# Seven block products for a third group's output, and the weight sums on GpSimd issued earlier

## The chip, the cores and the metric

The kernel runs on one core of one Trainium2 chip. The metric is the device time of one execution in microseconds (us), taken as the median of repeated runs. Engines are named as the profile names them: PE is TensorE (matmul; PEld its weight loads), DVE is VectorE, ACT is ScalarE, POOL is GpSimd, SP is the engine that issues most DMAs.

## The reference

A gated linear attention over 4 batches, 8 heads, 768 positions and a head width of 48, whose output, seen as 3072 tokens of 384 values, goes through an RMS norm and a gated expert layer with 1536 hidden values:

```python
state = np.zeros((B, H, D, D))
for t in range(S):
    state = alpha[:, :, t, :, None] * state + np.einsum('bhd,bhe->bhde', k[:, :, t], v[:, :, t])
    y[:, :, t] = np.einsum('bhd,bhde->bhe', q[:, :, t], state)
x = y.transpose(0, 2, 1, 3).reshape(B * S, H * D)          # (3072, 384)
xn = x / np.sqrt(np.mean(x * x, axis=-1, keepdims=True) + 1e-06) * rms_g
g = xn @ w_gate                                            # (3072, 1536)
out = (g * (1 / (1 + np.exp(-g))) * (xn @ w_val)) @ w_out  # (3072, 384)
```

## The kernel before

**Tiling.** The 3072 tokens are cut into 24 chunks of 128 (number cc; six per batch, the four batches in turn), and the chunks into seven groups of 4, 2, 2, 4, 4, 4 and 4 (`GROUPS`, numbered 0 to 6). Every float32 product is made of three float16 matmuls (`SPLIT`): each operand is split into a high half and the rest, and high x high, high x rest and rest x high are added up in PSUM.

**Stages.** `attention(cc)` does one chunk. VectorE scans the decay forward and back (L730), and multiplies k and q with the scans (L753, L760). The halves are made by ScalarE (high) and VectorE (rest: L808 for q). PE makes the score matrix `at2`. VectorE masks it (L886), ScalarE takes its high half `a16`, and VectorE the rest (L911, `al` in the plan). PE adds the chunk's y from the state (L924) and from the scores (L941), and the new state sums (L959). VectorE scales y by the norm's gains (L1001), GpSimd takes the root of the norm (L997, tile `ss`, one tiny instruction per chunk), and the split x is turned by a DMA. `decode` brings one block of the weights, which arrive as 64-bit floats, into float16 halves; six blocks i0 to i11 (gate and value) and o0 to o5 (output) make up 18 in all. A name in `SIGN_H` has its sign bits copied by ScalarE and one VectorE instruction at L544 in place of two at L531 and L536; a name in `LOW_W` has its rest made by PE and ScalarE instead of VectorE. `inspect` loads blocks once more and checks their range.

**The expert layer.** `expert_in(g, f)` makes 128 of the 1536 hidden values (step f, twelve of them) of a group: 9 matmuls for the gate and 9 for the value (L1215, 512 columns wide for a group of four chunks), SiLU on ScalarE, the gating on VectorE (L1232), the split on ScalarE and VectorE (L1245). `expert_out` makes the output of groups 0 to 4: per chunk 12 x 3 matmuls of 384 columns (L1593), so 144 for a group of four. Groups 5 and 6 (`FAST`) use `fast_out`: the product of h (512 x 1536) and w_out (1536 x 384) as 2 x 2 blocks with seven block products in place of eight (L1474), 252 matmuls of 192 columns for a group. For that, `mix(g, i)` makes sums and differences of the halves of two h tiles on VectorE (L1297 to L1326: per pair of steps five instructions of 256 columns and one of 512 more than the plain split) and `mix_out(i)` makes sums of w_out's blocks on GpSimd: nine instructions for each of six blocks, 54 in all (L1384, L1390, L1393, L1403; five of the nine are 384 wide, four are 192 wide; their tiles are `kh_t`, `qp_t` and the results `raw_T` and `wu_T`).

**Order.** A planner lists all operations with their dependences, and each engine issues its own in the order that the number table `PLACE` gives. Nothing moves at run time: an instruction whose operands are late holds all that stand behind it on its engine. `BUFS` says how many buffers each name has. `WARM` and `FILL` are numbers of filler matmuls at the start.

Of the kernel before, what the change touches and what calls it, by code (L numbers as in the profile page):

```python
# [8 lines left out]
F16 = mybir.dt.float16  # L9
F32 = mybir.dt.float32  # L10
# [46 lines left out]
SIGN_H = ["i0", "i1", "i2", "i4", "i5", "i6", "i7", "i8", "i9", "i10", "i11", "o0"]  # L57
REST_A = ['i0', 'i1', 'i2', 'i4']
WARM = 11
FILL = 16  # L60
LOW_W = ["i6", "o1", "o2"]

BUFS = dict(
    att=3, v=2, ss=2, kh=2, qp=2, k16=2, q16=2, kT=2, v16=4, gd=2, a16=2, s16=2, dk=1, x32=1, x16=2,
    xT=2, raw=4, wu=2, h16=13, sl=2, h32=3, ob=2, at2=1, y=2, mm=4,
# [3 lines left out]
    rg=0.7, resta=1.06, warm=6.4, fill=0.22, hneg=0.23, hr=0.5,  # L69
    ss=0.12, kh2=0.68, scu=1.1, st2=0.34, scan1=0.6, xs=0.5, xh=0.45, xless=0.17, xr=0.46, kid=0.98, kTh=0.65, kTl=0.53, xid=0.88, xTl=0.47, kneg=0.23, kr=0.45,  # L70
# [5 lines left out]
    neg=0.48, wneg=0.2, wl2=0.38,  # L76
# [19 lines left out]
9 0 5 30 8 v 2b 6 2 3 1b u 2f w 11 2c 3a 1 4 7 c h 1l f g i l j p n 13 16 z 14 1c 1k 1o 1q 1w 21 27 2e 2i 2l 18  # L96
1d 1f a b k r x 10 y 12 17 15 1e 1i 1m 1u 1y 24 25 28 2g 2m 2t 2v 2z 1r 1v 1x d q 19 1g 2o 1h 1j 20 1n 1t 22 2a
2r 2w 3i 3l 3q 3g 42 49 4f 2k 32 38 s 2d 8w 2s 2x 3o 31 35 3d 3n 4a 3h 3r 3v 3z 44 46 4c 4l 4t 4y 51 4r 5n 67 t
36 3p 3u 40 45 o 2u 34 39 3e 3k m 1z 26 2j 2p 2y e 1p 1s 23 2h 2n 29 3t 3w 41 4b 4p 2q 4i 4m 53 58 5r 3y 4z 52
54 5b 5l 6q 6t 5d 5q 6b 70 3f 64 6c 6p 6v 72 4q 5z 61 69 6h 6m 6w 82 85 8f 8l 92 59 6y 7g 7n 7y 86 5h 78 7b 7h  # L100
7o 7s 7l 8y 94 9e 9i 9p 6f 7d 7w 7z 8n 8z 96 9c 84 8h 8p 9d 7q 8m 8u 9f 9z a7 aa ae a3 a5 ac al 8s a4 a6 ab ag
ay 8k 9s af ak an b9 9j b0 b4 bh bm bq 4e 4j 4s 5a 5f 5k 3s 43 48 4d 4h 57 33 37 3b 3j 5j 5m 3c 47 3m 4g 4k 4u
4x 50 55 5p 6s 6u 56 6l 5e 6z 76 79 5c 5o 5t 5v 63 6d 5i 5u 5x 68 7e 7j 6i 6r 6n 7f 83 8b 6e 77 74 7p 7t 89 5y
62 6a 6k 6o 75 7i 7r 7u 8j 99 9m 81 87 8c 91 9r a0 6x 7a 7k 80 8e 98 97 9l 9o 9w ah bf 8r 90 93 9g 9v bl 8g ai
8v bd bg bx 9t 9x a2 ad ap b2 b7 bc bi bp by c5 cc cg ds mq co cr c9 cf cl ct dc gr 1a 4n 3x 4o 5s 4w 5w 5g 8i
at 73 7c 7x av az 9a 9k 9n 9q aj b6 b8 bb bn br bv c0 c1 c6 c7 cb cd ci aw bt c2 cn 4v 71 60 66 65 6g 8q 8d 8x
9b a1 ao 8o 95 9h 7m 88 8a 8t am aq 9u 9y a8 ar au ax ba be bk bo bs bw bz c3 b5 cz d8 dg d3 d9 db dm e5 e8 d0
# [36 lines left out]
1au 1b0 1b3 19q 19y 19z 1a6 1a5 1a8 1ad 1ac 1ag 1ai 1ao 1aa 1an 1al 1az 1b4 1bh 1bu 1c3 1cd 1a4 1a9 1ae 1aj 1ap
1ar 1aw 1as 1av 1ay 1bd 1ax 1b2 1b5 1b8 1b1 1bj 1b7 1bb 1bc 1ba 1bf 1bg 1be 1bm 1bl 1bq 1br 1bp 1bt 1bs 1bw 1du
1bv 1cp 1dw 1bx 1c8 1dy 1ak 1bi 1at 1bo 1bn 1by 1c2 1cc 1bz 1c0 1c1 1c5 1c6 1c7 1ca 1c9 1cv 1cg 1cs 1d1 1d3 1cl
1cm 1co 1ce 1cr 1cu 1d5 1c4 1cb 1ci 1cj 1ch 1d7 1dc 1dn 1cf 1ck 1cn 1cx 1cw 1cz 1de 1d2 1dg 1dl 1dp 1d0 1d6 1df
1dk 1dm 1dr 1eg 1em 1eu 1cq 1ct 1da 1dd 1cy 1d4 1d8 1di 1dv 1dx 1e3 1dz 1ee 1e5 1e8 1dq 1ds 1e4 1ef 1eh 1db 1dh
1dj 1eb 1do 1dt 1e0 1e2 1ej 1el 1en 1eq 1f6 1es 1ex 1e9 1ez 1eo 1et 1ev 1e1 1e6 1e7 1ep 1ec 1ei 1ek 1f1 1f3 1f5
# [6 lines left out]
class Plan:  # L156
# [21 lines left out]
    def order(self):  # L178
# [9 lines left out]
        for o in done:  # L188
# [11 lines left out]
            if o["lock"]:  # L200
                port, owner = t + (0.1 if o["lock"] == 2 else cost), e
# [145 lines left out]
def tile_attn_moe(  # L347
# [1540 lines left out]
```

## Time and profile before

| | us |
|---|---|
| three runs | 505.33, 504.17, 505.94 (median 505.33) |
| the profiled execution, its own time | 504.43 |
| its span in the trace | 502.7 |
| PE busy | 494.9 |
| VectorE busy | 426.4 |
| ScalarE busy | 290.8 |
| GpSimd busy | 75.6 |

The span runs from the first to the last instruction that the profiler records; 1.7 us of the execution lie outside it. The rows that are read from this execution stand in a section below.

### The profile page before, as it was taken

The page shows a single profiled execution, that of the slowest core. Times are in us where ns is not written, and L with a number is a line of the kernel's source. Part 1 is how long each engine was busy: PE and PEld are TensorE (multiplying, and loading weights), DVE is VectorE, ACT ScalarE, POOL GpSimd, SP SyncE. Part 2 cuts the span into 40 slices and gives each one's busy share as a digit, 9 for nine tenths or more (in the row PEclk, how much of TensorE's full clock was granted, in tenths as well). Part 3 has the DMA queues.
Part 4 walks back from the last instruction along what each step waited for, and adds up shares of the span by engine and source line. Part 5 has one row for each costly group of instructions (what it writes and reads, how often), then busy time and mean ns, then how long its engine had stood idle before and what let it go on. Part 6 is the DMA issues. An engine that isn't in the chain of part 4 may idle for free.

```text
span 502.7 us, 13364 instructions
## 1 busy us (share of the span) xinstructions
PE 494.9 (98%) x5483; PEld 319.1 (63%) x5483; DVE 426.4 (85%) x805; ACT 290.8 (58%) x793; POOL 75.6 (15%) x109
## 2 busy tenths in 40 slices
PE   8999999999999999999999999999999999999996
PEld 4888645668968875555566555454654568744496
DVE  8999999999999999997999788997777882256853
ACT  2687888446645663375473457466657574276730
POOL 3200000010000010001011100759473120000000
PEclk9999999999999999999999999999999999999999
DMA  8999763650583449373163816250512064234002
GB/s 240 328 271 257 234 230 106 165 131 22 93 183 100 107 95 207 87 114 81 22 137 104 198 54 177 54 158 1 158 65 78 33 173 126 103 128 148 1 2 67
DMA packets 66002, 63.33 MB, mean 126 GB/s; under 512 B 33984, under 2 KB 60064, under 8 KB 65936
## 3 DMA queue, kind: packets, MB, share of 16 engines
q1 hardware_dynamic: 65504, 62.14, 47.4%
q8 instruction: 43, 0.70, 0.6%
q10 hardware_dynamic: 432, 0.30, 0.2%
q14 instruction: 23, 0.19, 0.1%
HBM read 49.84 MB, written 4.72 MB: 109 GB/s over the span
## 4 chain that ended last, share of the span: by engine, by line
PE 93%; DVE 2%; DMA 1%; issue 0%; ACT 0%; SPq 0%; ACTq 0%
PE mm L1215 56%; PE mm_po L1593 19%; PE at L865 3%; PE y L941 2%; PE mm_w_Z L1474 2%; PE y L924 2%; PE mm_w_Y L1474 2%; PE at_w_XY L1474 1%; DMA raw_i<-w_val 1%; PE mm_w_X L1474 1%; PE y_w_Y L1474 1%; PE mm_u L959 1%; PE at_u L959 1%; PE y_w_X L1474 1%; DVE dk L730 1%; PE y L935 0%
## 5 line engine op out<-in xcount | busy, mean ns | idle before, releaser
L1215 PE MATMUL mm<-xT,wg 128*128 128x512 f16 (+1 forms) x1602 | 290.8, 338 | 0.2 <-DVE wg L576 0.2
L1215 PEld LDWEIGHTS <-wg 128*128 128x128 f16 x1602 | 154.1, 98 | 118.4 <-DVE wg L576 0.6
L1593 PE MATMUL mm_po<-wo,h 128*128 128x384 f16 x576 | 98.6, 326 | 0.0
L1593 PEld LDWEIGHTS <-h 128*128 128x128 f16 x576 | 55.2, 98 | 36.7
L1226 ACT ACTIVATE sl<-mm 128x512 f32<-128x512 f32 (+1 forms) x89 | 44.8, 507 | 46.2 <-PE mm L1215 38.4
L1232 DVE SCALAR_TENSOR_TENSOR h<-mm,sl 128x512 f32<-128x512 f32 (+1 forms) x89 | 51.6, 583 | 20.8 <-PE mm L1215 11.6
L499 ACT ACTIVATE h<-h 128x512 f16<-128x512 f32 (+1 forms) x89 | 48.1, 541 | 24.3 <-DVE h L1232 16.6
L997 POOL TENSOR_TENSOR ss<-ss,mhalf 128x1 f32<-128x1 f32 x24 | 18.8, 786 | 278.6 <-ACT ss L994 219.1
L730 DVE TENSOR_TENSOR_SCAN dk<-att,seed 112x520 f32<-112x520 f32 x47 | 58.6, 1246 | 1.0 <-ACT dec L741 0.3
L1245 DVE TENSOR_TENSOR h<-h,h 128x512 f16<-128x512 f32 (+1 forms) x89 | 52.4, 601 | 4.2 <-ACT h L499 4.0
L886 DVE TENSOR_TENSOR at<-at,mask 128x1024 f32<-128x1024 f32 x20 | 24.5, 1225 | 7.0 <-PE at L865 7.0
L908 ACT CAST a<-at 128x1024 f16<-128x1024 f32 x20 | 20.1, 1005 | 14.6 <-DVE at L886 14.6
L1474 PEld LDWEIGHTS <-h 128*128 128x128 f16 x288 | 23.9, 98 | 1.1 <-issue 0.4
L911 DVE TENSOR_TENSOR a<-at,a 128x1024 f16<-128x1024 f32 x19 | 23.1, 1214 | 0.6 <-ACT a L908 0.5
L988 ACT ACTIVATE junk<-y 128x384 bf16<-128x384 f32 x24 | 11.6, 484 | 20.7 <-PE y L941 17.1
L941 PE MATMUL y<-v,a 128*128 128x48 f16 x480 | 23.5, 184 | 0.0
L924 PE MATMUL y<-s,q 112*128 112x96 f16 x240 | 22.9, 205 | 0.0
L499 ACT ACTIVATE att_X<-dk_hs 128x256 f16<-128x256 f32 (+1 forms) x24 | 12.3, 514 | 14.1 <-DVE dk_hs L1309 10.3
L941 PEld LDWEIGHTS <-a 128*128 128x128 f16 x480 | 19.4, 96 | 0.0
L1038 ACT ACTIVATE x<-x,ss 128x384 f16<-128x384 f32 x21 | 12.8, 608 | 9.7 <-DVE x L1001 6.9
L834 ACT CAST s<-sd 48x192 f16<-48x192 f32 x40 | 13.7, 344 | 8.1 <-DVE sd L826 7.6
L657 ACT ACTIVATE raw_s<-raw_s 128x768 f32<-128x768 f32 x18 | 16.4, 912 | 3.1 <-DVE raw_s L653 3.1
(197 smaller groups left out, 678.8 us busy)
## 6 DMA issues: line engine op xcount, KB each, us to landing
att<-att SPq DMA_DIRECT2D x22, 675.9 KB, 5.7
v<-vtok SPq DMA_DIRECT2D x24, 192.0 KB, 3.3
raw_i<-w_gate SPq DMA_DIRECT2D x12, 384.0 KB, 7.3
raw_i<-w_val SPq DMA_DIRECT2D x12, 384.0 KB, 7.9
raw_o<-w_out SPq DMA_DIRECT2D x6, 768.0 KB, 4.8
raw_s<-w_gate SPq DMA_DIRECT2D x12, 384.0 KB, 3.3
raw_s<-w_val SPq DMA_DIRECT2D x12, 384.0 KB, 4.1
raw_s<-w_out SPq DMA_DIRECT2D x6, 768.0 KB, 5.2
```

The lines of the kernel that those rows point to most:

```text
L499: nc.scalar.activation(dst, src, AF.Copy, scale=scale, accum_out=stat[:rows, col : col + 1])
L730: nc.vector.tensor_tensor_scan(out, x, start.rearrange("r g p c -> r (g p c)"), 0.0, op0=ALU.mult, op1=ALU.add)
L886: nc.vector.tensor_tensor(x, x, mask[:, :, 1:].to_broadcast([P, NP, 2, C]), op=ALU.mult)
L911: nc.vector.tensor_tensor(a_tile()[:, :, 1], t["sc"], a_tile()[:, :, 0], op=ALU.subtract)
L924: nc.tensor.matmul(yps[:, 2 * p * D : 2 * (p + 1) * D], t["q16"][:, x, p, :], s16_tile()[:, y, p].rearrange("r j e -> r (j e)"), start=p = ...
L941: nc.tensor.matmul(out_y, a_tile()[:, j, x, p, :], t["v16"][:, y, p, j, :], start=False, stop=m == 2, skip_group_check=True,)
L1215: nc.tensor.matmul(ps[:, :n], wg[:, f, x, j, kk, :], xT[:, y, kk, cs], start=i == 0, stop=i == 3 * NK - 1,)
L1226: nc.scalar.activation(t["sl"][:, :n], t[0][:, :n], AF.Silu, scale=1.0 / (S_X * S_W))
L1232: nc.vector.scalar_tensor_tensor(t["h"][:, :n], t[1][:, :n], S_H / (S_X * S_W), t["sl"][:, :n], op0=ALU.mult, op1=ALU.mult,)
L1245: nc.vector.tensor_tensor(h16_of(g, f)[:, 1, cs], t["h"][:, :n], h16_of(g, f)[:, 0, cs], op=ALU.subtract)
L1474: nc.tensor.matmul(out, left(a, i, x, c), right(b, i, y), start=m in LAST and i == 0 and n == 0, stop=i == NPR - 1 and n == 2, skip_group_ ...
L1593: nc.tensor.matmul(t[i, c][:, : c[1] - c[0]], h16_of(g, f)[:, x, ts], wo[:, f // 2, y, f % 2, c[0] : c[1]], start=f == 0 and m == 0, stop= ...
```

## The change

- `FAST` takes in group 4: its output comes from seven block products (252 matmuls of 192 columns) in place of 144 of 384 columns, and its h goes through `mix`. The gating of a step in a mixed group waits for the gating of the last step of the other parity, which the planner now knows.
- The 54 sums of `mix_out` stand much earlier in the order of GpSimd and are costed by the planner in another way (`HOLD`).
- `SIGN_H` takes in o1 to o5; `LOW_W` takes in i0.
- Buffers: `v` 2 to 1, `v16` 4 to 2, `x16` 2 to 1, `raw` 4 to 5, `wu` 2 to 3. v of the first four chunks lies in tiles of k16 and q16; the mixed halves lie in `wu` instead of `dk`, and `raw` instead of `att`; the checks of the mixed groups load into `att`.
- Two fillers fewer (11 + 16 to 12 + 13). The first six range checks stand with group 3 instead of 4. All numbers of `PLACE` are new. `LOW_P` and `H_P` are empty, so their branches do nothing.

```diff
-SIGN_H = ["i0", "i1", "i2", "i4", "i5", "i6", "i7", "i8", "i9", "i10", "i11", "o0"]
+SIGN_H = ['i0', 'i1', 'i2', 'i4', 'i5', 'i6', 'i7', 'i8', 'i9', 'i10', 'i11', 'o0', 'o1', 'o2', 'o3', 'o4', 'o5']
-WARM = 11
-FILL = 16
-LOW_W = ["i6", "o1", "o2"]
+WARM = 12
+FILL = 13
+LOW_W = ['i0', 'i6', 'o1', 'o2']
 BUFS = dict(
-    att=3, v=2, ss=2, kh=2, qp=2, k16=2, q16=2, kT=2, v16=4, gd=2, a16=2, s16=2, dk=1, x32=1, x16=2,
-    xT=2, raw=4, wu=2, h16=13, sl=2, h32=3, ob=2, at2=1, y=2, mm=4,
+    att=3, v=1, ss=2, kh=2, qp=2, k16=2, q16=2, kT=2, v16=2, gd=2, a16=2, s16=2, dk=1, x32=1, x16=1,
+    xT=2, raw=5, wu=3, h16=13, sl=2, h32=3, ob=2, at2=1, y=2, mm=4,
 )
-FAST = [5, 6]
+FAST = [4, 5, 6]
-CHECK = [(4, f) for f in range(0, 12, 2)] + [(5, f) for f in range(12) if f % 3] + [(6, f) for f in range(4)]
+CHECK = [(3, f) for f in range(0, 12, 2)] + [(5, f) for f in range(12) if f % 3] + [(6, f) for f in range(4)]
+HOLD = 0.22
 PLACE = """
...
@@ load_v
-        v = buf(ap, [P, DM], F32, "v16", cc) if cc < NB else buf(ain, [P, DM], F32, "v", cc)
+        if cc < NB:
+            v = buf(ap, [P, NP, C], F32, v_home(cc), cc).rearrange("p a c -> p (a c)")[:, :DM]
+        else:
+            v = buf(ain, [P, DM], F32, "v", cc)
@@ expert_in
+        before = [halves_of_h[1 - f % 2][6]] if g in FAST and (f or g - 1 in FAST) else []
-        h = op("DVE", c_h, gate, [p1, sl], [b1, s_k, h_k])
+        h = op("DVE", c_h, gate, [p1, sl, *before], [b1, s_k, h_k])
@@ mix
-        hs_k, x_k = ("dk", ("hs", g, i)), ("att", ("X", g, i // 2))
+        hs_k, x_k = ("wu", ("hs", g, i)), ("raw", ("X", g, i // 2))
-        free = mixed[g, i - 1]["W"][:1] if i else state_ops[NC - 1]["qp"]
+        free = mixed[g, i - 1]["W"][:1] if i else []
@@ mix_out
-        o = add("POOL", "tsp", lambda: diff(0), [w_ops["o", i]] + after, [d0], lock=True)
+        o = add("POOL", "tsp", lambda: diff(0), [w_ops["o", i]] + after, [d0], lock=3)
...
```

The order on GpSimd, before, around the first of the 54 sums (`ss` is the root of a chunk's norm, with the chunk's number; `kh_t_0`, `qp_t_0` are the sums of block o0):

```order
L997 TENSOR_TENSOR ss_12_4198<-ss_12_4198,mhalf_117 128x1
L997 TENSOR_TENSOR ss_13_4281<-ss_13_4281,mhalf_117 128x1
L997 TENSOR_TENSOR ss_15_4778<-ss_15_4778,mhalf_117 128x1
L1384 TENSOR_TENSOR kh_t_0_4803<-wo_134 128x384
L997 TENSOR_TENSOR ss_14_4824<-ss_14_4824,mhalf_117 128x1
L1384 TENSOR_TENSOR qp_t_0_4974<-wo_134 128x384
L1390 TENSOR_TENSOR kh_t_0_4803<-kh_t_0_4803,qp_t_0_4974 128x384
```

The same engine in the changed kernel, from chunk 2's root on:

```order
L1022 TENSOR_TENSOR ss_2_482<-ss_2_482,mhalf_117 128x1
L1022 TENSOR_TENSOR ss_3_564<-ss_3_564,mhalf_117 128x1
L1411 TENSOR_TENSOR kh_t_0_986<-wo_134 128x384
L1411 TENSOR_TENSOR qp_t_0_1031<-wo_134 128x384
L1417 TENSOR_TENSOR kh_t_0_986<-kh_t_0_986,qp_t_0_1031 128x384
L1420 TENSOR_TENSOR qp_t_0_1031<-wo_134,kh_t_0_986 128x192
L1420 TENSOR_TENSOR qp_t_0_1031<-wo_134,qp_t_0_1031 128x192
L1430 TENSOR_TENSOR raw_T_0_1133<-kh_t_0_986,raw_T_0_1133 128x384
```

The first sum moves from behind the roots of chunks 12, 13 and 15 to behind that of chunk 3. In the changed order 14 sums stand ahead of chunk 5's root, 39 ahead of chunk 7's and 53 ahead of chunk 12's.

The order on VectorE, before, up to the rest of chunk 12's scores (`a16_12`; `dk`, `qp`, `kh`, `at2` are tiles of `attention`, with the chunk's number):

```order
L730 SCALAR_TENSOR_TENSOR dk_14_3603<-att_14_2831,seed2_95 112x520
L760 TENSOR_TENSOR qp_14_3654<-att_14_2831,dk_14_3603 112x2x4x64
L753 TENSOR_TENSOR kh_14_3658<-att_14_2831,dk_14_3603 112x2x2x64 x2
L886 TENSOR_TENSOR at2_12_3538<-at2_12_3538,mask_102 128x1024
L839 TENSOR_TENSOR s161_144<-sd0_136,s161_144 48x4x48
L730 SCALAR_TENSOR_TENSOR dk_15_3680<-att_15_3428,seed_91 112x520
L808 SCALAR_TENSOR_TENSOR q16_13_3635<-qp_13_3587,q16_13_3635 112x512
L735 RECIPROCAL seed2_95<-dk_15_3680 112x8
L730 SCALAR_TENSOR_TENSOR dk_15_3680<-att_15_3428,seed2_95 112x520
L911 TENSOR_TENSOR a16_12_3678<-at2_12_3538,a16_12_3678 128x2x512
```

The same place in the changed kernel:

```order
L755 SCALAR_TENSOR_TENSOR dk_13_3619<-att_13_2756,seed_91 112x520
L911 TENSOR_TENSOR at2_12_3564<-at2_12_3564,mask_102 128x1024
L760 RECIPROCAL seed2_95<-dk_13_3619 112x8
L755 SCALAR_TENSOR_TENSOR dk_13_3619<-att_13_2756,seed2_95 112x520
L1066 SCALAR_TENSOR_TENSOR x16_11_3648<-x32_11_3615,ss_11_3617,x16_11_3648 128x384
L864 TENSOR_TENSOR s161_144<-sd0_136,s161_144 48x4x48
L824 SCALAR_TENSOR_TENSOR v16_12_3630<-v_12_3470,v16_12_3630 128x384
L936 TENSOR_TENSOR a16_12_3663<-at2_12_3564,a16_12_3663 128x2x512
```

Before, VectorE has done the scans of chunks 13, 14 and 15 by the time it comes to `a16_12`; in the changed order it has done those of chunk 13 alone. VectorE has 26 instructions fewer ahead of `a16_12`, and PE has 63 matmuls of 512 columns fewer ahead of chunk 12's y.

On PE, the 144 products of 384 columns that stood among the last steps of group 4 and the first of group 5 are gone, and 252 of 192 columns stand there; the first 45 of them lie between the gate and the value of group 5's first step.

## Rows read from the trace of the kernel before

**Rows 1.** The page: busy time, and VectorE's busy tenths in 40 slices.

```profile
PE 494.9 (98%) x5483; PEld 319.1 (63%) x5483; DVE 426.4 (85%) x805; ACT 290.8 (58%) x793; POOL 75.6 (15%) x109
...
DVE  8999999999999999997999788997777882256853
```

**Rows 2.** PE's waits: line waited for, us in total, times, longest us.

```profile
PE mm_busy L1659 <- POOL minus L446: 1.7, 1, 1.7
...
PE mm L1215 <- DVE wg L576: 0.2, 1, 0.2
```

**Rows 3.** Windows: stretch, then PE, PEld, DVE, ACT, POOL busy, PEclk, DMA share, GB/s.

```profile
0.00:41.30 41.30, 37.57 (x408) 29.44 (x409) 38.57 (x57) 25.70 (x55) 7.92 (x29) 1.00 0.93 269
41.30:206.00 164.70, 164.70 (x2069) 116.22 (x2067) 161.69 (x319) 101.70 (x289) 7.13 (x8) 1.00 0.60 148
...
255.00:410.00 155.00, 155.00 (x1628) 84.81 (x1626) 130.81 (x228) 93.96 (x260) 58.54 (x70) 1.00 0.38 102
```

**Rows 4.** Timeline of PE: start us, us, instructions.

```profile
355.83 2.10 PE L1215 MATMUL mm<-xT,wg 128*128 128x512 f16 x9
357.77 8.94 PE L1593 MATMUL mm_po<-wo,h 128*128 128x384 f16 x54
366.55 1.67 PE L1215 MATMUL mm<-xT,wg 128*128 128x512 f16 x7
...
486.56 1.65 PE L1474 MATMUL at_w_XY<-wo,h 128*128 128x192 f16 x18
488.04 1.15 PE L1474 MATMUL at_w_XY<-raw_T,att_X 128*128 128x192 f16 x12
```

**Rows 5.** Timeline of VectorE and PE: chunk 12's scores and its y.

```profile
204.78 1.20 DVE L911 TENSOR_TENSOR a<-at,a 128x1024 f16<-128x1024 f32 x1
...
211.03 0.29 PE L924 MATMUL y<-s,q 112*128 112x96 f16 x3
```

**Rows 6.** VectorE's groups by shape: line, shapes, count, then busy us, mean ns.

```profile
L730 DVE TENSOR_TENSOR_SCAN dk<-att,seed 112x520 f32<-112x520 f32 x47 | 58.6, 1246 | 1.0 <-ACT dec L741 0.3
L1245 DVE TENSOR_TENSOR h<-h,h 128x512 f16<-128x512 f32 x55 | 38.8, 714 | 4.2 <-ACT h L499 4.0
...
L760 DVE TENSOR_TENSOR qp<-att,dk 112x512 f32<-112x512 f32 x24 | 17.2, 715 | 1.0 <-POOL raw_T L1403 0.8
...
L808 DVE SCALAR_TENSOR_TENSOR q<-qp,q 112x512 f16<-112x512 f32 x20 | 14.4, 719 | 0.6 <-ACT q L499 0.6
...
L1305 DVE TENSOR_TENSOR h<-h,h 128x256 f32<-128x256 f32 x12 | 5.1, 425 | 0.4
...
L536 DVE SCALAR_TENSOR_TENSOR raw_o<-raw_o 128x768 int32<-128x768 int32 x5 | 4.8, 962 | 0.1
...
L815 DVE SCALAR_TENSOR_TENSOR gd<-dec 112x4 f32<-112x4 f32 x20 | 4.0, 204 | 0.0
L544 DVE TENSOR_SCALAR wu_i<-raw_i 128x768 int32<-128x768 int32 x7 | 3.9, 552 | 0.0
...
L531 DVE TENSOR_SCALAR raw_o<-raw_o 128x768 int32<-128x768 int32 x5 | 2.8, 565 | 0.0
```

**Rows 7.** Timelines of GpSimd and VectorE where sums run beside VectorE's work.

```profile
260.05 0.54 DVE L815 SCALAR_TENSOR_TENSOR gd<-dec 112x4 f32<-112x4 f32 x1
...
334.68 0.92 POOL L1384 TENSOR_TENSOR kh_t<-wo 128x384 f32<-128x384 f16 x1
...
344.40 1.00 POOL L1390 TENSOR_TENSOR kh_t<-kh_t,qp_t 128x384 f32<-128x384 f32 x1
...
334.76 1.39 DVE L760 TENSOR_TENSOR qp<-att,dk 112x512 f32<-112x512 f32 x1 [0.81 <-POOL raw_T L1403]
336.07 0.68 DVE L1245 TENSOR_TENSOR h<-h,h 128x512 f16<-128x512 f32 x1
...
344.30 1.17 DVE L911 TENSOR_TENSOR a<-at,a 128x1024 f16<-128x1024 f32 x1
...
404.45 1.40 DVE L1321 TENSOR_TENSOR att_X<-dk_hs,att_X 128x512 f16<-128x512 f32 x1
```

More of the change, by code (lines that the diff above doesn't have):

```diff
@@ L75 @@
     sadd=0.36, tsp=0.9, ttp=0.6, th=0.62, us=0.35, uo=0.32,
[L76 removed]
+    wlp=1.85, vlp=0.95, hlp=1.25, neg=0.48, wneg=0.2, wl2=0.38,
 )
@@ L153 @@
+1g5 1g6 1g9 1g8 1gd 1gn 1gt 1go 1gv 1gx 1h2 1h4 1gz 1h9 1gw 1h0 1gy 1h5 1hb 1gi 1gp 1gr 1h6 1gu 1h1 1h3 1hf 1hd
+1hh 1hn 1hj 1hl 1hp 1hs 1hk 1hr 1i2 1i5 1i7 1h8 1hc 1hi 1hm 1hq 1ht 1hv 1hy 1hw 1i6 1hx 1i4 1hz 1ie 1i0 1i1 1i3
+1i9 1is 1i8 1ic 1id 1iw 1ib 1ih 1ij 1ig 1it 1iu 1il 1in 1io 1iq 1im 1iy 1j0 1ir 1ix 1iz 1iv 1j1 1j2 1hg 1hu 1ia
+1if 1ii 1ik 1ip 1j4 1j3
 """
@@ L200, in order @@
             if o["lock"]:
-                port, owner = t + (0.1 if o["lock"] == 2 else cost), e
+                port, owner = t + {2: 0.1, 3: HOLD * cost}.get(o["lock"], cost), e
             o["t"] = t
@@ L573, in high, with scaled, low_p @@
             nc.scalar.activation(dst[:, 0], word().bitcast(F32), AF.Copy, scale=scale)
+        def scaled():
+            w = word().bitcast(F32)
+            nc.scalar.activation(w, w, AF.Copy, scale=scale)
+        def low_p():
+            nc.gpsimd.tensor_tensor(dst[:, 1], word().bitcast(F32), dst[:, 0], op=ALU.subtract)
         def low():
@@ L633, in decode, with inspect @@
         o = add("ACT", "wh", high, [o], [wu])
+        if name in LOW_P:
+            o = add("ACT", "wh", scaled, [o], [wu])
+            return add("POOL", "wlp", low_p, [o], [wu], lock=3)
         return add("DVE", "wl", low, [o], [wu], lock=True)
-    def inspect(src, dst, name, col, after):
+    def inspect(src, dst, name, col, after, home):
         t = {}
         def load():
-            raw = buf(wst, [P, NW], I64, "raw", name)
+            if home == "raw":
+                raw = buf(wst, [P, NW], I64, "raw", name)
+            else:
+                raw = buf(ain, [P, AW + AW % 2], F32, "att", name)[:, : 2 * NW].bitcast(I64)
             for i, ap_in in enumerate(src):
@@ L1074, in attention @@
         la = la[1:]
-        v_k = key("v16" if first else "v")
+        v_k = key(v_home(cc) if first else "v")
         lv = op("SP", 0.45, lambda: load_v(cc), [prev.get("lv")], [v_k], kb=196)
@@ L1139, in attention @@
                 al = add("DVE", "al", a_lo, [a16], [at0, key("a16")])
-        ins = [key("a16"), key("v16"), key("y")] + ([] if first else [key("q16"), key("s16")])
+        ins = [key("a16"), v_k if first else key("v16"), key("y")] + ([] if first else [key("q16"), key("s16")])
         y0 = add("PE", "y0" if first else "y", lambda: output(0), [al, vl or lv, sl], ins)
@@ L1170, in back @@
                 state_ops[cc]["st"] = add("DVE", "st" if first else "st2", s_front, [st], ku)
-            ins = [key("kT"), key("v16"), *ku]
+            ins = [key("kT"), v_k if first else key("v16"), *ku]
             if joined:
@@ L1276, in expert_in @@
         else:
-            hl = op("DVE", c_h, h_lo, [hh], [h_k, o_k], lock=True)
+            p = g in H_P
+            hl = op("POOL" if p else "DVE", 2 * c_h + 0.03 if p else c_h, h_lo, [hh], [h_k, o_k], lock=3 if p else True)
         h_ops.setdefault((g, f), []).append(hl)
@@ L1408, in mix_out @@
         d0, d1 = d_k
-        o = add("POOL", "tsp", lambda: diff(0), [w_ops["o", i]] + after, [d0], lock=True)
-        o = add("POOL", "tsp", lambda: diff(1), [o], [d1], lock=True)
-        o = add("POOL", "tsp", both, [o], [d0, d1], lock=True)
+        o = add("POOL", "tsp", lambda: diff(0), [w_ops["o", i]] + after, [d0], lock=3)
+        o = add("POOL", "tsp", lambda: diff(1), [o], [d1], lock=3)
+        o = add("POOL", "tsp", both, [o], [d0, d1], lock=3)
         h0 = add("ACT", "th", lambda: t_top(0), [o], [d0, k])
@@ L1417, in mix_out @@
             o = add(
-                "POOL", "ttp", lambda n=n, a=a, b=b, f=f: more(n, a, b, f), [o], [d0, d1], lock=True
+                "POOL", "ttp", lambda n=n, a=a, b=b, f=f: more(n, a, b, f), [o], [d0, d1], lock=3
             )
         h1 = add("ACT", "th", lambda: t_top(1), [o], [d1, k])
-        l0 = add("POOL", "tsp", lambda: t_low(0), [h0], [d0, k], lock=True)
-        t_ops[i] = add("POOL", "tsp", lambda: t_low(1), [h1, l0], [d1, k], lock=True)
+        l0 = add("POOL", "tsp", lambda: t_low(0), [h0], [d0, k], lock=3)
+        t_ops[i] = add("POOL", "tsp", lambda: t_low(1), [h1, l0], [d1, k], lock=3)
         sums_of_w.extend((h0, h1))
@@ L1706, in tile_attn_moe @@
                 i = unchecked.pop(0)
-                sums_of_w.append(inspect(w_src[i], w_dst[i], f"s{i}", o_w + i, step))
+                sums_of_w.append(inspect(w_src[i], w_dst[i], f"s{i}", o_w + i, step, "att" if g in FAST else "raw"))
         if g in FAST:
```

135 lines of the change are left out of this document (69 added, 66 removed).

## The prediction, made before the changed kernel ran

> **What bounds the kernel now.** I read the page first: PE is busy 494.9 of 502.7 us, 98%, and VectorE 426.4; VectorE's slices stand at 9 from the second to the eighteenth and fall off only later [rows 1]. Then PE's waits: the list has five entries, 3.5 us in all, from the 1.7 us for the first constants to the 0.2 us for a weight block, and all five lie in the start [rows 2]. So behind the start the time is the number of PE's columns times what a column costs, and only what takes columns away, or makes PE wait, shows. The windows tell where a new wait could come from: from 41.3 to 206 us PE is busy for 164.70 of 164.70 us, and so is VectorE for 161.69, which leaves it 3.0 us; from 255 to 410 us VectorE is busy for 130.81 of 155.00, and most of GpSimd's work lies there, 58.54 us against 7.13 in the stretch before [rows 3]. The granted clock is 1.00 in each of these. The sum is made against the profiled execution, 504.43 us (span 502.7), which is 0.9 under the median of 505.33; the result is compared with the median, so a difference goes onto both.
>
> **PE's own work: -2.5 us.** The timeline gives the pitch of a product of 384 columns: 54 from 357.77 to 366.55, 162.6 ns each. Of 192 columns: 18 from 486.56 to 488.04, 82.2 ns. Of 512: nine from 355.83 to 357.77, 215.6 ns [rows 4]. The fifth group's output loses 144 x 0.1626 = 23.4 us and gains 252 x 0.0822 = 20.7, which is -2.7: the products are an eighth fewer columns (252 x 192 against 144 x 384), and nothing of that is lost to the shorter form, for which the price is within 1.1% of half. i0's rest on PE adds four products of 384 columns, +0.65. Two fillers fewer give -0.43 if they are as long as two of the 512-column products; at 41.3 us both orders have done eight expert steps, and the start I leave equal within 0.7 for its new loads and buffers. Net -2.5, which is all that can be won.
>
> **VectorE, later.** Mixing the fifth group's h adds, per pair of steps, five instructions of 256 columns at 0.425 at most and one of 512 at 0.714 [rows 6]: 6 x 2.84 = 17.0 as an upper end, and about 0.9 for the smaller evictions. It falls between 255 and 410 us, where VectorE has 155.00 - 130.81 = 24.2 us idle [rows 3] and loses the sums as neighbours. Free, then; without that cover, each us would be one of PE's. The first block products need the mixed halves: behind group 4's last step stand the gate of group 5's first step (nine products) and then 45 products, 3.7 us, before pair 5's first is needed.
>
> **The sums on GpSimd: the term that decides.** All 54 leave the stretch from 259 to 407 us, and by the new order 53 stand ahead of chunk 12's root. Until there VectorE has no idle time. What a sum costs VectorE the trace does show. At 334.76 the product of q with its scan takes 1.39 beside the sum at 334.68, where its kind takes 0.715; the next instruction, at 336.07, takes 0.68 and pays nothing; the small one at 260.05 takes 0.54 against 0.204; the one at 404.45 takes 1.40 where others of its form take 0.714 [rows 6, 7]. Counted so, each against the lower quarter of its kind, 24 of the 71 VectorE instructions that a sum overlaps are longer by 0.12 to 0.72 us, the first at 260.05 and the last at 404.45, 11.3 us in all: 0.21 per sum. Those that read PSUM pay nothing: the one at 344.30 takes 1.17 beside the sum at 344.40 [rows 7]. The mean takes in sums that ran where VectorE had little to do; the 24 sums in stretches of 4 us with VectorE over 95% busy cost 0.28 each. A wide sum never cost more than 0.72, nor a narrow one more than 0.36, so with five wide and four narrow per block the top is 0.55 per sum, 29.7 us for 54. The bottom is 0, if every sum meets instructions that read PSUM. I take 0.25, between the two means and nearer to the busy one: 54 x 0.25 = 13.5 us.
>
> The Trainium skill's page "SBUF — State Buffer", section "Who interferes with whom", says that a VectorE instruction with two inputs in SBUF and a GpSimd instruction that reads SBUF share a port, and that whoever issues first keeps the other out fully. The rows agree on who is spared (344.30) and on the size of the worst case (334.76); that 47 of 71 pay nothing they don't decide, since GpSimd's own sums get longer too. If each sum kept VectorE out for its whole turn, the sum would go by the top.
>
> **The room that VectorE has.** I work it out at chunk 12's y, where it is least. Before, the rest of its scores starts at 204.78 and ends at 205.98, and PE comes to the y at 211.03 [rows 5]: 5.0 us of room. In the changed order PE comes there with 63 products of 512 columns fewer (-13.6), i0's four (+0.65) and two fillers less (-0.43): 13.4 earlier, at 197.6. VectorE has 26 instructions fewer ahead of it: four scans of 1.246 (4.98), two products of 0.715 (1.43), fifteen smaller ones, 5.5 together (each between the 0.204 of the small row and 0.719), and the signs of five output blocks, each of which gives one instruction of 0.552 for two of 0.565 and 0.962, -4.88, and i0's rest, -0.77 [rows 6]. That is 17.6 by means; starts overlap by about 0.08, so 15.5: ready at 190.5. Room: 197.6 - 190.5 = 7.1 us, or 10.1 if the 3.0 us of VectorE's waits [rows 3] go too; I take 8.6. The collisions want 13.5. **PE waits 4.9 us for VectorE**, in some chunk before the thirteenth, and once lost it doesn't come back. -2.5 + 4.9 = +2.4: 506.8 against 504.43, 507.7 against the median; I write 507.5.
>
> **Edits costed at nothing.** The five sign copies go to ScalarE, busy for 101.70 of 164.70 us there [rows 3]. `v` and `x16` with one buffer make loads and turns wait for a reader; the cover is the chunk's lead (the y's room above), and the DMA share is 0.60 in that stretch. Without the lead, a late v would hold VectorE's `v_lo` and all behind it. The new homes only change which tiles a buffer waits for. The first six checks move with their loads from group 4 to group 3, behind other loads on SP, where PE needs nothing of them. The gate's extra wait is for an instruction that the same engine issued earlier.
>
> **The rivals.**
> - *A, the forecast:* the sums outgrow VectorE's room by 1.5 to 5 or so more than PE wins, 506.9 to 510.8. For it: the 3.0 us of idle time, and the price of a busy stretch. Against it: the room is worked out with two unlike ends.
> - *B, gain eaten:* a sum costs 0.17 to 0.23, so 9 to 12.5 against 8.6, and PE waits 1 to 4 us: 503.8 to 506.8, about 505.3. For it: the mean of 0.21.
> - *C, faster:* the sums wait for GpSimd's turn rather than VectorE for them. The place is the stretch 67 to 200 us, the price of a sum there 0.16 or less, so that 54 stay under the 8.6 of room; GpSimd has no other work there (7.13 of 164.70 us), so its sums may grow as they like. Then PE is never kept waiting: 505.33 - 2.5 = 502.8. For it: 47 of 71 that paid nothing, and the free PSUM readers, which in that stretch are many.
> - *D, the full lock:* each sum costs its top: 29.7 - 8.6 - 2.5 = +18.6, 524. Against it: 0.28 even where VectorE was over 95% busy. It is what the Trainium skill's page "SBUF — State Buffer" would make of it with GpSimd always first.
> - *E, the fifth group's mixing comes late* at its first block product: 2 us or 3 over C or A, some 505 to 510; 24.2 us of idle time and 3.7 us of other products speak against it.
> - That the change doesn't do what it says: 192-column products at more than 82.2 ns. At 92.9 the gain would be gone; the last group's 252 speak against it.
>
> **How the numbers follow.** A 0.38, B 0.25, C 0.33, D 0.02, E 0.02. A measurement of this kernel can tell about 0.3%, 1.5 us, from no change: 503.8 and 506.85 are the bounds. Faster is C, 0.33. Within is B, 0.25. Slower is A, D and E, 0.42. The likeliest case gives 507.5. The range goes from C's 502.8 less 0.3 for the start, 502.5, to the 510.8 of A's upper end (a sum at 0.31: 16.8 - 8.6 - 2.5 = +5.7); D lies outside. Since both signs hold much of it: A's own range is 506.9 to 510.8.
>
> **What would show it.** In the changed profile: PE's busy time about 492.5, the 252 new products at 82 ns each, and no wait after 255 us. PE's waits should have new entries between 67 and 206 us on the scores and y of `attention`, released by VectorE, of 4 to 8 us together with what shows as slow products; VectorE's instructions with two SBUF inputs should be 0.7 longer where sums lie, about a third of them, 13 us in all. If the lengthenings come to under 9 us and PE has no waits, it is C. If the lengthenings are as large as I say and PE still has no waits, the room was larger than I worked out. If PE waits for a DMA, or waits at the block products, the forecast is wrong even where the time is right.

## The result, and the profile after

The changed kernel takes 511.9 us (median of four runs, 510.87 to 513.22), the kernel before 504.85 beside it: a ratio of 1.0137, 95% interval 1.0118 to 1.0155, or 7.05 us more. The forecast was slower, and the mechanism that it named shows in the profile, but the time lies above the range's 510.8. The profiled execution is the longest of the four: 513.22 us, span 511.5, so 8.8 over before's.

The page of the changed kernel, busy time and slices, answers to [rows 1]:

```profile
PE 494.9 (97%) x5593; PEld 326.6 (64%) x5593; DVE 436.5 (85%) x842; ACT 303.6 (59%) x829; POOL 85.0 (17%) x109
...
DVE  7999999997999999999999999997469973277752
...
POOL 3320066364372423010000000100000000000000
PEclk9999999998999999999999999999999999999999
```

GpSimd's work now lies mostly in slices 6 to 16 (64 to 205 us), beside a VectorE at 9. In the tenth slice (115 to 128 us) VectorE falls to 7 and the granted clock is below full. PE's waits [rows 2], by line, total, times and longest, had been five with 3.5 us; now they are ten with 10.0:

```profile
PE at_u L984 <- DVE st L1007: 2.2, 1, 2.2
PE mm L1240 <- DVE h L1257: 1.9, 3, 1.3
PE mm_busy L1686 <- POOL minus L458: 1.7, 1, 1.7
PE at L872 <- DVE qp L785: 1.5, 1, 1.5
...
PE at_w_XY L1501 <- DVE ob L1522: 0.5, 1, 0.5
```

The 2.2 us stand at 115 us; those on h (L1257 is L1232 before) at 69, 72 and 173; a wait of 0.4 for `gd` at 175; the one on `ob` at 493. Those on qp and the constants lie in the start. The windows of [rows 3] read now:

```profile
0.00:41.30 41.30, 36.01 (x399) 28.18 (x400) 38.14 (x56) 25.68 (x56) 10.69 (x29) 1.00 1.03 267
41.30:206.00 164.70, 160.14 (x2095) 114.89 (x2093) 160.23 (x297) 109.24 (x309) 63.95 (x61) 0.99 0.50 136
...
255.00:410.00 155.00, 154.86 (x1773) 93.16 (x1771) 134.00 (x269) 90.11 (x253) 5.58 (x8) 1.00 0.33 88
```

PE, which had never stopped between 41.3 and 206 us, is idle there for 4.6: the five waits from 69 to 175 us. Behind 255 us it is as full as before, and VectorE takes the fifth group's mixing in its gaps, as forecast.

**Where it collides.** The stretch ahead of the longest wait, VectorE first (start, us, instructions), then GpSimd:

```profile
107.26 1.03 DVE L851 TENSOR_TENSOR sd<-st,gd 112x192 f32<-112x192 f32 x1
108.22 0.68 DVE L833 SCALAR_TENSOR_TENSOR q<-qp,q 112x512 f16<-112x512 f32 x1
108.82 0.19 DVE L760 RECIPROCAL seed<-dk 112x8 f32<-112x8 f32 x1
108.94 1.28 DVE L792 TENSOR_TENSOR k<-kh,k 112x512 f16<-112x512 f32 x1
110.14 0.61 DVE L1066 SCALAR_TENSOR_TENSOR x<-x,ss,x 128x384 f16<-128x384 f32 x1
110.67 1.94 DVE L755 TENSOR_TENSOR_SCAN dk<-att,seed 112x520 f32<-112x520 f32 x1
112.54 0.99 DVE L851 TENSOR_TENSOR sd<-st,gd 112x192 f32<-112x192 f32 x1
...
108.64 1.03 POOL L1430 TENSOR_TENSOR raw_T<-qp_t,raw_T 128x384 f16<-128x384 f32 x1 [0.56 <-ACT raw_T L511]
109.63 1.88 POOL L1411 TENSOR_TENSOR kh_t<-wo 128x384 f32<-128x384 f16 x1
111.48 1.84 POOL L1411 TENSOR_TENSOR qp_t<-wo 128x384 f32<-128x384 f16 x1
113.40 1.46 POOL L1417 TENSOR_TENSOR kh_t<-kh_t,qp_t 128x384 f32<-128x384 f32 x1
```

Seven sums, from 106.6 to 115.6 us, stand beside a scan of 1.94 instead of 1.246 [rows 6], two decays of the state of 1.03 and 0.99 instead of about 0.35, a product of 1.28 instead of 0.68. GpSimd's own instructions take 1.84 to 1.88 where they took 0.92 [rows 7]: both engines are slower beside each other. Over all 54 sums VectorE's instructions are longer by 13.7 us, counted as in the prediction: 0.255 per sum, where 0.25 was taken. A rival would be the norm's root, which GpSimd now does behind sums, and for which VectorE might be kept waiting. The list of VectorE's own waits speaks against it: from 60 to 206 us it has three lines, none of them for GpSimd, and the first is for PE:

```profile
DVE h L1257 <- PE mm L1240: 2.9, 2, 2.6
```

**What a wait brings with it.** Windows of 1 us behind the wait at 115 us; the third number from the end is PE's granted clock:

```profile
115.00:116.00 1.00, 0.00 (x0) 0.00 (x0) 1.00 (x3) 0.13 (x1) 0.55 (x1) 1.00 0.87 225
116.00:117.00 1.00, 0.00 (x0) 0.00 (x0) 1.00 (x5) 0.86 (x3) 0.00 (x0) 1.00 1.26 228
117.00:118.00 1.00, 0.82 (x49) 0.80 (x50) 1.00 (x2) 0.00 (x0) 0.00 (x0) 0.57 0.80 149
118.00:119.00 1.00, 1.00 (x7) 0.69 (x7) 0.82 (x5) 0.93 (x3) 0.00 (x0) 0.50 0.92 309
119.00:120.00 1.00, 1.00 (x6) 0.75 (x5) 0.00 (x0) 0.95 (x4) 0.00 (x0) 0.50 1.05 297
120.00:121.00 1.00, 1.00 (x9) 0.78 (x7) 0.00 (x0) 0.97 (x4) 0.00 (x0) 0.73 1.03 235
```

PE stood still, and then ran at the lower of its two levels (0.50 is 1.2 of 2.4 GHz) for some 3 us: 0.43 + 0.50 + 0.50 + 0.27 = 1.7 us lost in addition to the wait. VectorE, late a moment before, then stands idle and waits for PE (the 2.6 us above).

**The sum.** For each profile I took the time at which PE gets to a point, less the products done by then at the median pitch of their shape, fillers counted as no work: what is left is PE's loss. Its level depends on the pitches, so only differences are read.

| PE's loss, us | to 60 | 60 to 206 | 206 to 485 | to its last product |
|---|---|---|---|---|
| before, two profiles | 14.6, 14.6 | 6.35, 6.36 | 6.1, 6.1 | 0.10, 0.10 |
| changed | 15.2 | 13.8 | 5.95 | 0.76 |
| changed, again | 17.5 | 11.95 | 6.1 | 0.76 |
| sums late (first experiment) | 15.0 | 7.35 | 21.6 | 0.74 |
| sums as memsets | 16.4 | 7.33 | 5.3 | 0.79 |
| first 27 as memsets | 15.5 | 8.4 | 5.4 | 0.80 |
| last 27 as memsets | 14.9 | 11.3 | 5.6 | 0.78 |
| signs back on VectorE | 14.9 | 16.2 | 6.4 | 0.74 |
| first 27 later | 15.85 | 8.3 | 11.8 | 0.75 |

PE's work itself falls by 1.75 at these pitches, which are whole nanoseconds (83 for 192 columns, 162 for 384); at the 82.2 and 162.6 of [rows 4] it falls by 2.05. So the 8.8 us between the two profiled executions are -1.75 + 0.6 + 7.45 - 0.15 + 0.65, and 2.0 behind PE's last product (6.1 us to the end of the span against 4.1).

The two middle columns have to be read together, since what a late PE hasn't done by 206 us counts in the next one. From 60 to 485 us PE's loss is 12.45 before, 12.63 with the sums as memsets, which read nothing (an experiment below), and 18.05 in the changed kernel's second profile, in which the clock was full there: the sums cost PE 5.4 us, the new order without them 0.2. (Counted at the same products instead of the same times, the sums cost 5.5.) The first profile has 19.75, of which 1.7 is the clock.

The 2.0 us at the end go with one issue of a DMA. SyncE's last issue of an output block takes 1.94 us in the changed kernel's profile; in six profiles of the change and its variants it takes 1.8 to 1.9, and the end is the long one; in the other five, and in both of before, it takes 0.43, and the end is the short one. The changed kernel, then the first run under "The end" (e3_tail):

```profile
503.72 1.94 SPq L1528 DMA_DIRECT2D out_dram<-ob  x1
```

```profile
503.30 0.43 SPq L1528 DMA_DIRECT2D out_dram<-ob  x1
```

Why it is slow in some, no run shows.

### The profile page after: what moved, and what is told of

Read it like the earlier page. It is cut to its first block, busy times and chain, and to the rows that moved or that the text cites. A ratio compares the mean times of both kernels' runs of the same rounds, so it can differ in the third digit from the quotient of the medians.

```text
span 511.5 us, 13672 instructions
## 1 busy us (share of the span) xinstructions
PE 494.9 (97%) x5593; PEld 326.6 (64%) x5593; DVE 436.5 (85%) x842; ACT 303.6 (59%) x829; POOL 85.0 (17%) x109
## 4 chain that ended last, share of the span: by engine, by line
PE 63%; DVE 3%; issue 1%; DMA 1%; ACT 0%; ACTq 0%; DVEq 0%
PE mm L1240 39%; PE mm_po L1620 7%; PE mm_w_Y L1501 3%; PE mm_w_Z L1501 3%; PE mm_w_X L1501 2%; PE y L966 2%; PE y L949 2%; PE at L890 1%; PE at_w_XY L1501 1%; PE y_w_Y L1501 1%; PE mm_u L984 1%; DMA out_dram<-ob 1%; PE y_w_X L1501 1%; DVE dk L755 0%; DVE a L936 0%
## 5 line engine op out<-in xcount | busy, mean ns | idle before, releaser
L1620 PE MATMUL mm_po<-wo,h 128*128 128x384 f16 x432 | 73.6, 326 | 0.0
L1257 DVE SCALAR_TENSOR_TENSOR h<-mm,sl 128x512 f32<-128x512 f32 (+1 forms) x89 | 51.3, 580 | 25.0 <-PE mm L1240 20.4
L1022 POOL TENSOR_TENSOR ss<-ss,mhalf 128x1 f32<-128x1 f32 x24 | 20.8, 867 | 243.5 <-ACT ss L1019 231.9
L1620 PEld LDWEIGHTS <-h 128*128 128x128 f16 x432 | 41.6, 98 | 27.8 <-issue 0.4
L1501 PEld LDWEIGHTS <-h 128*128 128x128 f16 x432 | 35.9, 98 | 1.0
L1501 PEld LDWEIGHTS <-raw_X 128*128 128x128 f16 x324 | 26.9, 98 | 1.9 <-issue 1.3
L511 ACT ACTIVATE raw_X<-wu_hs 128x512 f16<-128x512 f32 (+1 forms) x36 | 18.5, 515 | 7.6 <-DVE wu_hs L1336 5.4
L859 ACT CAST s<-sd 48x192 f16<-48x192 f32 x40 | 13.8, 346 | 11.3 <-DVE sd L851 7.3
```

The costliest lines, as they stand in the source:

```text
L511: nc.scalar.activation(dst, src, AF.Copy, scale=scale, accum_out=stat[:rows, col : col + 1])
L1257: nc.vector.scalar_tensor_tensor(t["h"][:, :n], t[1][:, :n], S_H / (S_X * S_W), t["sl"][:, :n], op0=ALU.mult, op1=ALU.mult,)
L1501: nc.tensor.matmul(out, left(a, i, x, c), right(b, i, y), start=m in LAST and i == 0 and n == 0, stop=i == NPR - 1 and n == 2, skip_group_ ...
L1620: nc.tensor.matmul(t[i, c][:, : c[1] - c[0]], h16_of(g, f)[:, x, ts], wo[:, f // 2, y, f % 2, c[0] : c[1]], start=f == 0 and m == 0, stop= ...
```

## The experiments

In the first experiment and in "The first half later", `PLACE` is renumbered for the operations named, and scratch of the sums moved lies in `wu`, which is free there. The code shown is cut; three dots stand for what is left out.

**The sums elsewhere.** The 54 sums behind 206 us:

```diff
 PLACE = """
...
+        if i < 4:
+            d_k = (("wu", ("t", i)),) * 2
...
```

> The changed kernel with its 54 weight sums on GpSimd (and their 12 ScalarE copies) moved from 67-205 us to two later stretches, about 206-275 us (blocks o0 to o3) and 340-365 us (o4, o5). Theory (the sums lengthen VectorE's instructions where VectorE has no room, and PE waits for it): PE's waits between 60 and 206 us go, 7 us less than the changed kernel's 511.9, so 504 to 506. Rival 1 (the new order, the single buffers of v and x16, or the new loads cause the waits): 510 or more, with the same waits at about 72, 115 and 174 us. Rival 2 (the waits follow the sums, since VectorE is busy for 48.6 of 49 us from 206 to 255 as well): 508 to 511, with new waits behind 206 us.

522.14 us, ratio 1.0338 (1.0286 to 1.0391). The first window below (60 to 206 us) shows PE without a pause; the second and third show the price. Then four lines of its waits, all behind 206 us:

```profile
60.00:206.00 146.00, 146.00 (x2103) 104.45 (x2101) 136.45 (x285) 90.11 (x256) 5.88 (x8) 1.00 0.49 119
206.00:350.00 144.00, 137.44 (x1617) 74.84 (x1616) 142.16 (x254) 91.49 (x260) 56.34 (x55) 1.00 0.42 108
350.00:485.00 135.00, 129.94 (x1054) 82.36 (x1053) 86.02 (x169) 67.22 (x185) 10.56 (x18) 0.97 0.30 90
```

```profile
PE y L949 <- DVE s L864: 2.1, 3, 1.3
PE mm L1240 <- DVE h L1257: 1.9, 2, 1.3
PE mm_w_X L1506 <- DVE h L1270: 1.7, 1, 1.7
PE mm_w_Y L1506 <- POOL wu_T L1435: 1.7, 1, 1.7
```

The waits at 72, 115 and 174 us go with the sums, so they were the sums'. But the theory's time was wrong by 16 us and more. The second rival was right on the place, new waits behind 206 us, and also far too low on the time: VectorE is as full there, and the last blocks came too late for the block products (`wu_T`). From 206 to 485 us PE's loss is 15.5 us over before's: 11.5 of waits, and 3.4 by a granted clock of 0.50 from 356 to 363 us.

**The sums without their reading.**

```diff
-            nc.gpsimd.tensor_tensor(t[0], t[0], t[1], op=ALU.add)
+            nc.gpsimd.memset(t[0], 0.0)
...
```

> The changed kernel with each of the 54 sums replaced by a memset of the same tile and shape at the same place in GpSimd's order: GpSimd still writes, but reads nothing (the sums' values are left out of the output). Theory (VectorE and GpSimd collide on reading): VectorE's instructions beside them keep their usual length (under 2 us lost in all, against 13.7), the waits of PE between 60 and 206 us go, 504 to 506. Rival (order, buffers or loads): 510 or more. If writing alone also collides: 508 to 511 with lengthened VectorE instructions.

506.33 us (ten runs), ratio 1.0007 (0.9977 to 1.0037): no difference from before that the runs can tell, and 0.3 above the theory's range. VectorE's busy time falls from 436.5 to 424.0; of the 44 instructions that a memset overlaps none is longer than its kind by anything that counts, 0.15 us in all. PE never stops from 60 to 206 us, and VectorE has 9.9 us idle there:

```profile
60.00:206.00 146.00, 146.00 (x2103) 104.51 (x2100) 136.10 (x281) 96.92 (x282) 22.12 (x60) 1.00 0.49 119
```

One reservation: the memsets are also shorter (19.2 us for 54 against 59.2). That a VectorE instruction with two inputs in SBUF doesn't collide with a GpSimd instruction which only writes there is what the Trainium skill's page "SBUF — State Buffer", section "Who interferes with whom", states, and the 0.15 us agree. The second thing follows from the time: with the collisions gone the change still gains nothing.

**Which sums.** Half of the sums are memsets, so these kernels too leave out values. The condition is `i in (0, 1, 3)` for the blocks that come first, `i in (2, 4, 5)` for the last:

```diff
+            if i in (0, 1, 3):
+                nc.gpsimd.memset(t[0], 0.0)
+            else:
                 nc.gpsimd.tensor_tensor(t[0], t[0], t[1], op=ALU.add)
...
```

> The changed kernel with the 27 sums of the blocks that come first (o0, o1, o3, about 66 to 130 us) as memsets, which read nothing; the other 27 (about 122 to 205 us) as they are. The output lacks the memset sums' values. Theory (VectorE has some 8 us of room by then, and 27 sums at 0.25 us want 6.8): no wait of PE before 206 us beyond those of the all-memset kernel, so 505.5 to 507. Rival (each sum costs PE its share wherever it stands): halfway between the all-memset kernel's 506.3 and the changed kernel's 511.9, 509.

> The changed kernel with the 27 sums of the blocks that come last (o2, o4, o5) as memsets, and those of o0, o1, o3 (about 66 to 130 us) as they are. The output lacks the memset sums' values. Theory (early in that stretch VectorE has the least room, so the first sums make the waits): PE's waits at about 72 and 115 us stay, the one at 174 us goes, 509.5 to 511. Rival (each sum costs its share wherever it stands): 509. If the room is the same for both halves: 506 to 507, as the other half.

507.29 us with the first 27 free (1.0026, 1.0001 to 1.0051), 511.31 with the last 27 free (1.0104, 1.0063 to 1.0145): each 0.3 above its theory's range. The same window, first and last free in turn, and the waits of the latter:

```profile
60.00:206.00 146.00, 145.17 (x2075) 103.88 (x2077) 138.26 (x277) 96.01 (x279) 40.61 (x60) 1.00 0.48 118
```

```profile
60.00:206.00 146.00, 142.20 (x1991) 101.90 (x1990) 140.62 (x275) 93.93 (x273) 45.27 (x61) 1.00 0.47 114
```

```profile
PE at_u L984 <- DVE st L1007: 2.2, 1, 2.2
...
PE mm L1240 <- DVE h L1257: 1.5, 2, 1.3
```

The halves are not alike, as the theories had it: the first 27 lengthen VectorE's work by 8.8 us (0.33 each) and cost PE 4.3 from 60 to 485 us against the memset kernel, the last 27 lengthen it by 4.4 (0.16 each) and cost 1.2. That the last 27 make no wait was wrong: two of 0.4, at 168 and 170 us, are theirs.

**More VectorE work at the same place.**

```diff
-SIGN_H = ['i0', 'i1', 'i2', 'i4', 'i5', 'i6', 'i7', 'i8', 'i9', 'i10', 'i11', 'o0', 'o1', 'o2', 'o3', 'o4', 'o5']
+SIGN_H = ['i0', 'i1', 'i2', 'i4', 'i5', 'i6', 'i7', 'i8', 'i9', 'i10', 'i11', 'o0']
```

> The changed kernel with the signs of o1 to o5 back on VectorE, so 4.9 us more VectorE work in the stretch in which the weights are decoded (before 206 us), and five ScalarE copies fewer. Theory A (VectorE's total sets PE's waits in that stretch: each us is one of PE's): 516 to 517. Theory B (the waits come from bunches of lengthened instructions at single places, and elsewhere there is room): 512 to 514.

515.7 us, ratio 1.0194 (1.0142 to 1.0247), 3.8 over the changed kernel (3.4 if each is taken against the runs of before beside it), between the theories' numbers. PE's loss from 60 to 206 us is 16.2, at a granted clock of 1.00 throughout; against 11.95, which the changed kernel's second profile shows at the same clock, 4.9 us of VectorE's time cost PE 4.25. Its window shows VectorE with 2.4 us left:

```profile
60.00:206.00 146.00, 138.15 (x1888) 98.80 (x1886) 143.63 (x263) 87.48 (x262) 68.40 (x61) 1.00 0.42 107
```

**The first half later.**

```diff
 PLACE = """
...
+        if i in (0, 1, 3):
+            d_k = (("wu", ("t", i)),) * 2
...
```

> The changed kernel with the 27 sums of o0, o1 and o3 moved from 66-130 us to about 206-278 us (their scratch in a buffer that is free there), the other 27 as they are at 122-205 us; the output is whole. Theory (the early sums make the waits, because VectorE has least room there): PE's waits at 72 and 115 us go, those before 206 us are as in the kernel with the first sums as memsets, and what is left is what 27 sums cost from 206 to 278 us: none if VectorE's room has grown there, 507; at the rate at which 36 sums there cost in the first experiment (5.7 us of new waits), 511. If it is 507 this is the best place found; even so the kernel before, at 505, is not beaten, since the all-memset kernel was no faster than it.

512.22 us, ratio 1.0139 (1.0116 to 1.0161): no better than the change. The waits at 72 and 115 us are gone (8.3 against 8.4 with memsets), and 27 sums cost 6.4 us behind 206 (11.8 against 5.4):

```profile
206.00:255.00 49.00, 46.97 (x534) 23.83 (x523) 48.57 (x85) 26.33 (x76) 18.87 (x20) 1.00 0.57 145
255.00:300.00 45.00, 42.81 (x574) 24.55 (x573) 44.71 (x84) 27.77 (x78) 15.02 (x13) 1.00 0.43 108
```

VectorE is busy for 93.3 of 94 us there. VectorE's room is no larger there, and the 507 that it would have allowed is not reached; 511 was the other number expected.

**The end.** One VectorE chain ahead of the range verdict's work; one addition ahead of the products that write the same PSUM tile; then both, with the verdict's work behind that addition. Only numbers of `PLACE` change:

```diff
 PLACE = """
...
```

> The changed kernel with the last pair's difference W (one VectorE instruction, its ScalarE half and its VectorE rest) moved ahead of the range verdict's VectorE work near the end. Theory (the verdict's 2.3 us on VectorE hold that difference, and it holds ScalarE and VectorE before the first block products are put out): PE's waits at 493 us go, 0.7 to 1.3 us less, 510.6 to 511.2. Rival (the time behind PE's last product sets the end anyway): no difference, 511.9.

> The changed kernel with one VectorE instruction near the end (the first addition that puts out a block product of the last group) ahead of the PE products that write the other half of the same PSUM tile, as it stood before the change. Theory (it waits for those products only because it stands behind them, and the next products wait for it): the wait of PE at 493 us, 0.5 us, and the slow pair beside it go, so PE's products after 485 us end 0.6 us earlier in relation to their work; in the time 0.6 us, less than one run can tell. Rival: the wait stays.

> The changed kernel with both edits of the two experiments on the end, and the range verdict's VectorE work behind the first addition that puts out a block product. Theory (two links hold the end, and each experiment took away one): no wait of PE at 492 to 494 us, and its products after 485 us lose 0.3 us instead of 1.0. Rival (a third link, the copies on ScalarE): the wait of about 0.4 us stays.

The first made no difference (512.2 us, 1.0139, 1.0087 to 1.0191; the wait stayed at 0.5), the second moved the wait to the products before (0.4). With both it is gone. The second and third ran once each (510.96 and 511.81 us), so only their profiles are read. PE's products in the changed kernel, then in the last experiment:

```profile
491.91 1.65 PE L1501 MATMUL at_w_XY<-wo,h 128*128 128x192 f16 x18
494.06 1.15 PE L1501 MATMUL at_w_XY<-raw_T,raw_X 128*128 128x192 f16 x12 [0.50 <-DVE ob L1522]
```

```profile
491.60 1.65 PE L1501 MATMUL at_w_XY<-wo,h 128*128 128x192 f16 x18
493.08 1.15 PE L1501 MATMUL at_w_XY<-raw_T,raw_X 128*128 128x192 f16 x12
```

PE's loss at the end is 0.63 and 0.33 in the last two, against 0.76 and before's 0.10. So the new order there costs 0.65 us, of which the three moves give back 0.4.

**Once more, both kernels.**

> The kernel before, unchanged, for a second profile of its start. Up to 60 us the changed kernel and its variants lost 0.3 to 2.3 us more to waits of PE than the one profile of before. If the start of the change is worse by itself, this profile's loss lies within 0.3 us of the first one of before (14.6 us of time without products other than fillers by 60 us); if loads vary from run to run, it lies anywhere from 14.6 to 17.

> The changed kernel once more, for a second profile: the waits at 72, 115 and 174 us should be the same to 0.3 us, since they are made by the order; the granted clock behind the wait at 115 us may stay at 1.00 (in two of the variants with the same wait it did) or fall to about 0.5 for 3 us (as in two others), which makes 1.7 us of difference.

Before repeats to 0.05 us in each stretch. The changed kernel's waits at 72, 115 and 174 us repeat; the clock behind 115 us did not fall this time:

```profile
118.00:120.00 2.00, 0.57 (x49) 0.57 (x50) 2.00 (x6) 0.99 (x3) 0.00 (x0) 1.00 1.09 234
120.00:122.00 2.00, 2.00 (x22) 1.61 (x22) 1.07 (x5) 1.88 (x6) 0.00 (x0) 1.00 0.95 297
```

It fell in the start instead, to 0.50 from 19 to 26 us:

```profile
20.00:30.00 10.00, 10.00 (x95) 8.25 (x91) 7.85 (x12) 6.92 (x15) 0.81 (x1) 0.70 1.08 311
```

Its start loses 17.5 against 15.2; over the change and its variants the start lies from 14.9 to 17.5. The memset kernel's 16.4 also has a clock of 0.50 in it, from 14 to 17 us.

## Why the prediction was right or wrong

- *What bounds the kernel, and the place:* right. PE is the bound, VectorE in the saturated stretch is what makes it wait, and the moved sums are why: the waits go when the sums are moved away and when they read nothing.
- *The price of a sum:* right, 0.255 against 0.25. What was not seen is that it isn't even: 0.33 for the first 27, 0.16 for the last.
- *"PE waits 4.9 us":* right in size. The five waits add up to 4.5 us, and all of PE's loss that goes with the sums at full clock to 5.4 (18.05 against 12.63). Wrong in place: I put the least room at chunk 12's y. The waits come at 69, 72, 115, 173 and 175 us, where sums stand close together. At chunk 12's y VectorE is still in time: the rest of its scores ends at 204.65, and PE comes to the y at 205.61:

```profile
203.44 1.21 DVE L936 TENSOR_TENSOR a<-at,a 128x1024 f16<-128x1024 f32 x1
```

```profile
205.61 0.39 PE L949 MATMUL y<-s,q 112*128 112x96 f16 x3
```

- *"-2.5", what can be won:* 1.75 to 2.05. The two fillers (-0.43) are counted as no work here, and the start did not become shorter without them; no run took them away alone. The products cost 82 ns, as forecast. PE's busy time stayed at 494.9 where about 492.5 was forecast: it takes in the slow stretch behind 117 us (493.7 in e3_tail, in which the clock did not fall).
- *The step that failed is the sum itself:* it held the one wait and put everything else at nothing or near it. What was missing, against before: the clock that falls behind a wait (1.7 us, in about half of the executions: the four runs have a mean clock of 0.999 twice, with 510.87 and 511.15 us, and 0.995 twice, with 512.65 and 513.22); the start, "equal within 0.7" (0.3 to 2.9 worse); the end, not costed at all (0.65), where "no wait after 255 us" also failed, by the 0.5 at 493; and 0 to 2 us behind the last product. The new order from 60 to 485 us adds only 0.2. Together with 5.4 - 1.75 these give 4.8 at the least, for an execution in which clock, start and end are kind (5.4 - 1.75 + 0.2 + 0.3 + 0.65), and 6 us and more with the mean of the start (1.1) and one fall of the clock in two. The sum forecast 2.4.
- *Range:* its upper end took a dearer sum, but no second thing going wrong beside it. (505.33 + 5.7 is 511.0, not 510.8; the 511.9 lie above both.)
- *C, faster:* fell, and not by the price alone: with collisions gone altogether the kernel is as fast as before, not 2.5 us faster. In its profile the start loses 1.8 and the end 0.7 more than before's, and the time behind the last product is the long one.
- *D, the full lock:* fell. 13.7 us, not 29.7.
- *The edits costed at nothing:* the mixing of the fifth group is covered, as said (206 to 485 us: 5.95 of loss against 6.1). The signs moved to ScalarE are worth 3 to 4 us here, so without them the change would have stood near 515.7.

Open: what in the start makes it lose more and vary; why the clock falls behind the same wait in some executions only; and why SyncE's last issue is slow in some. No run took these apart. The clock is not the change's alone: of the 39 runs of the kernel before that stand beside the experiments, seven took 507.9 to 509.2 us at a mean clock of 0.988 to 0.990, and none of them was profiled. No version with the whole output beats the kernel before, and the memset kernel, in which the sums cost nothing, says why none with these parts was to be expected.

## What to carry to other kernels

Before work is moved onto an idle engine, count what it does to the neighbour with which it shares a path: here 0.25 us of VectorE for each sum that GpSimd reads from SBUF, and where the neighbour has no idle time, 2 us of work saved on the bound engine cost it 5.4 us of lost time. Measure the cover at every place where the bound engine meets the neighbour, not at the one where it looks least; work that comes in bunches is late at the bunch. And in a kernel whose bound engine never waits, a forecast of many small edits needs a term for the edits that are "free": here the start and the end lost 0.6 us each, and nothing was there to win it back.

## What the runs showed of the hardware

- The same wait of 2.2 us was followed by a granted clock of 0.50 for some 3 us in three profiles (the first of the change and two of its variants, e7_tail_order and e9_tail_all) and by full clock in two with the same order up to there (the change again, and e3_tail): 1.7 us for the same instructions.
- From the end of the last working instruction (ScalarE's, behind PE's last product) to the end of the span it took 2.7 to 3.0 us or 4.3 to 4.7 us, nothing between, over thirteen profiles. The long ones are those in which SyncE's last issue of an output block took 1.8 to 1.9 us in place of 0.43. Both profiles of the kernel before are in the lower group, both of the changed kernel in the upper.
- GpSimd's sums were lengthened as VectorE's instructions were: the first one took 2.91 us where its like took 0.92.

```profile
65.66 2.91 POOL L1411 TENSOR_TENSOR kh_t<-wo 128x384 f32<-128x384 f16 x1 [27.98 <-ACT wo L585]
```
